# Decode attention over 65,536 keys: K and V of a head in two transfers of 64 KB per partition instead of three, over a ring of 20 + 16 chunks

## The chip, the core and the metric

The kernel runs on one core of a Trainium2 chip. The metric is the time of one execution in microseconds (us); lower is better. The kernel before has a median of 657.81 us over three runs (657.35 to 657.81).

## What is computed

One token goes through a transformer layer: layer norm, attention of 32 query heads over 8 key/value heads with 65,536 cached positions each, an output projection with a residual, a second layer norm and a gated feed-forward part with a residual. All inputs are bf16.

```python
q = (x @ wq)                                            # [1, 512] @ [512, 4096]: 32 heads of 128
scores = einsum("bhqd,bhkd->bhqk", q, k) * 128 ** -0.5  # k_cache [8, 65536, 128]
o = einsum("bhqk,bhkd->bhqd", softmax(scores), v)       # v_cache [8, 65536, 128]
h = x + o.reshape(1, 1, 4096) @ wo
h2 = h + (sigmoid(n(h) @ w_gate) * (n(h) @ w_up)) @ w_down   # n: layer norm; 512 -> 1792 -> 512
```

K and V of one head are 16 MB each, so the caches are 8 x 32 MB of the 282.33 MB that the kernel reads.

## The kernel before, in words

**Chunks and blocks.** K or V of one head is 32 chunks. A chunk is 4 KB per partition (`TC` = 16 positions of 128 bf16 values on each of 128 partitions). A block is 8 chunks (`NC`), so a head has four blocks, r = 0 to 3.

**The ring and the pieces.** K and V share one buffer, `ring`, of 32 chunks per partition. A head's K and its V come in three pieces each: chunks 0 to 11, 12 to 19 and 20 to 31 (`PIECES`), that is transfers of 6, 4 and 6 MB, or 48, 32 and 48 KB per partition. `AT` gives each piece's place in the ring.

**The DMA queue.** The SP engine issues all these transfers from one program in a fixed order (`load`, line 329): for head h, K h.0, V h-1.0, V h-1.1, K h.1, K h.2, V h-1.2. Before each, SP waits until the ring chunks that it overwrites have been read. For K these marks are one-element memsets that VectorE (DVE) does between two transposes (line 514, `F{h}.0`, `F{h}.1`, `F{h}.3`); for V they are the ends of rounds of matmuls (`PV{h}.{r}`). A transfer that must wait holds up all that stand behind it.

**K on VectorE and TensorE.** DVE transposes each chunk in blocks of 32 x 32 from `ring` into one of eight slots of the key buffer `ktw` (line 511, named `T{b}.{c}`). A piece's first transpose waits for the whole piece. A transpose into a slot also waits for the four matmuls that read the slot's last content. TensorE (PE) multiplies four chunks at a time by the query columns (`S{b}.{c}`, through the helper of line 430), and the sums of a whole head stay in four PSUM banks. After the last block come the softmax's maxima (line 518), the exponentials on ScalarE (line 557), and four transposes of the probabilities on DVE into `PT_sb` (line 567). In DVE's program these four stand behind the next head's first eight chunk transposes (`A0`, then `A4`), and after them `B0`, two small steps for the softmax's denominators that need a result of PE.

**V on TensorE.** The product with V (`pv`, also line 430) is done for head h-1 while head h is scored: rounds of eight matmuls, one round for two chunks, in PE's program behind block 0 (10 rounds) and block 3 (6 rounds). When V rounds change from one piece to the next, PE's program branches away to wait for it and comes back (`waits`).

**Start and end.** First `wq` (4 MB) comes into ring chunks 24 to 31, then K of head 0; piece K0.2 overwrites `wq` and so waits for the query projection `q` (`project_q`, to 23.3 us). At the end, V of head 7 lies in other places (`V7`); `wo` goes into `ktw`, the last piece of V comes in 2 transfers (`LAST`: 8 chunks, then 4), and the feed-forward weights follow into the ring. The output needs, in a chain, the last rounds of V, the head's output, the last rows of `wo`, the layer norm, gate and up products, `hhT` (line 831) and the down product (line 836), whose weights `wd` are the last transfers.

Of the kernel before, what the change touches and what calls it, by code (L numbers as in the profile page):

```python
# [13 lines left out]
HKV = 8  # L14
# [3 lines left out]
D = 512  # L18
# [197 lines left out]
def bass_sequential_preLN__gqa_block_cached__glu_gated_glu__decode_kernel(  # L216
# [10 lines left out]
    CH = TC * DH  # L227
    PIECES = ((0, 12), (12, 20), (20, 32))
    RING = 32 * CH
    AT = {"K": (0, 0, 8), "V": (12, 24, 20), "K0": (0, 12, 20), "V7": (0, 12, 20), "wq": 24, "wg": 0, "wd": 7}  # L230
    NF = FF // 128
# [6 lines left out]
    with ExitStack() as es:  # L238
# [78 lines left out]
        W_AT = {"wg": AT["wg"] * CH, "wu": AT["wg"] * CH + 4 * FF}  # L317
        LAST = [(20, 28), (28, 32)]

# [3 lines left out]
        def load(k, h, q, deps, sem, name, cols=None):  # L323
# [6 lines left out]

        dma("sp", lambda e: e.dma_start(ring[:, AT["wq"] * CH:(AT["wq"] + 8) * CH].rearrange("p (k n) -> p k n", k=4),
                                        A_wq.rearrange("(p k) n -> p k n", p=128)), "r0", (), "wq")
        for q in range(3):
            load("K", 0, q, ["q"] if q == 2 else (), f"r{q + 1}", f"K0.{q}")
        for h in range(1, HKV):
            load("K", h, 0, ["F0.1" if h == 1 else f"F{h - 1}.3"], "ka", f"K{h}.0")
            load("V", h - 1, 0, ["F0.3" if h == 1 else f"PV{h - 2}.3:2"], "va", f"V{h - 1}.0")
            load("V", h - 1, 1, ["F0.4" if h == 1 else f"PV{h - 2}.3"], "vb", f"V{h - 1}.1")
            load("K", h, 1, [f"F{h}.0"], "ka", f"K{h}.1")
            load("K", h, 2, [f"F{h}.1", f"PV{h - 1}.0:4"], "kb", f"K{h}.2")  # L340
            load("V", h - 1, 2, [f"PV{h - 1}.0"], "vb", f"V{h - 1}.2")
        h = HKV - 1
        load("V", h, 0, [f"F{h}.3"], "va", f"V{h}.0")
        for i, (j0, nj) in enumerate(WO):
            src = A_wo[j0 * DH:(j0 + nj) * DH, :].rearrange("(p r) n -> p (r n)", r=nj)
            dst = ktw[:, j0 * D:(j0 + nj) * D]
            dma("sp", lambda e, src=src, dst=dst: e.dma_start(dst, src), f"wo{i}", [f"PV{h - 1}.3"] if i == 0 else (), f"wo{i}")
        load("V", h, 1, (), "vm", f"V{h}.1")
        for i, cols in enumerate(LAST):
            load("V", h, 2, (), ("vb", "vl")[i], f"V{h}.2{('', 'b')[i]}", cols)  # L350
        for k, w in (("wg", B_w_gate), ("wu", B_w_up)):
            src = w.rearrange("(p k) n -> p (k n)", p=128)
            for i, (k0, k1) in enumerate(W_SPLIT[k]):
                at = W_AT[k]
                dma("sp", lambda e, at=at, w=src, a=k0 * FF, z=k1 * FF: e.dma_start(ring[:, at + a:at + z], w[:, a:z]),  # L355
                    f"{k}{i}", [f"PV{HKV - 1}.0a"] if k == "wg" else (), f"{k}.{i}")
        src = B_w_down.rearrange("(p r) n -> p r n", p=128)
# [95 lines left out]
        def project_q(e):  # L453

            e.reg_mov(reg(e, 0), addr_of(xz, 8 + 7))
            e.reg_mov(reg(e, 4), addr_of(ring, AT["wq"] * CH))
            for kt in range(1, 4):
                e.reg_alu(reg(e, kt), reg(e, 0), 2 * 16 * kt, ALU.add)
                e.reg_alu(reg(e, 4 + kt), reg(e, 4), 2 * NQ * DH * kt, ALU.add)
            with e.Fori(0, HKV):  # L460
                for kt in range(4):
                    mm_at(e, ps(1, 0, 512, 0, 8), at_reg(xz, reg(e, kt), [[4 * 16, 128], [1, 8]]),
                          at_reg(ring, reg(e, 4 + kt), [[RING, 128], [1, 512]]), False, 32)
                for kt in range(4):
                    e.reg_alu(reg(e, kt), reg(e, kt), 2, ALU.subtract)
                for kt in range(4):
                    e.reg_alu(reg(e, 4 + kt), reg(e, 4 + kt), 1024, ALU.add)
            return e.matmul(ps(1, 0, 512, 0, 8), lhsT=qz[:, 0:8], rhs=qz[:, 0:512], start=False, stop=True, skip_group_check=True)
# [31 lines left out]
        def dve_block(b):  # L500
            h, r = b // NR, b % NR
            for c in range(NC):
                n, j = b * NC + c, r * NC + c
                q = sum(j >= z for _, z in PIECES)
                at = (first_chunk("K", h, q) + j - PIECES[q][0]) * CH
                src = ring[:, at:at + CH].bitcast(fp32)
                dst = ktw[:, (n % NKT) * CH:(n % NKT + 1) * CH].bitcast(fp32)
                deps = [f"K{h}.{q}"] if j == PIECES[q][0] else []
                if r or b == 0:
                    deps.append(f"S{b - 1}.{c}" if b else None)  # L510
                op("dve", lambda e, d=dst, sr=src: e.transpose(d, sr), deps, f"T{b}.{c}", to="T")  # L511
                mark = {7: 0, 11: 1, 23: 3}.get(j, 4 if h == 0 and j == 31 else None)
                if mark is not None:
                    op("dve", lambda e, m=4 * h + mark: e.memset(scr[:, m:m + 1], 0.0), (), f"F{h}.{mark}")
# [69 lines left out]

        PARTS = {0: 10, 3: 6}

        def pv(h, r, rounds=0):
            P.part["pe"] = ("B", (h, r, rounds))
            rounds, name = rounds or PARTS[r], f"PV{h}.{r}" + "a" * (rounds == 6)
            for k in range(2):  # L590
# [78 lines left out]
        def pe_flow(e, section):  # L669
# [8 lines left out]
            w0, p0 = addr_of(ktw, W0 + NC - 1 + 127), addr_of(PT_sb, 31 * 4)  # L678
            v_at = [addr_of(ring, j * CH) for j in AT["V"]]
            step = (2 * 2 * 512, 2 - 2 * 2 * 512)  # L680
            lag = v_at[0] - addr_of(ring, AT["V7"][0] * CH)
            i_last = v_at[0] - lag
            i_first = i_last + HKV * lag
# [4 lines left out]
            e.reg_mov(p, p0)  # L688
            e.reg_alu(v, i, v_at[0], ALU.min)
            goto("part")  # L690
# [12 lines left out]
            e.reg_mov(m, 6)  # L703
            e.reg_mov(k, 4)
            away("br_eq", w, w0, "values0", lambda: section("V0"), "sums")
            e.br_ne(w, w0 - 12, on_true="next", on_false="values3")
            label("values3")
            e.reg_mov(v, v_at[2])
            e.reg_mov(m, 4)
            e.reg_mov(k, 2)  # L710
            section("V3")
            goto("sums", "values")
            pv_regs(e)

            def last_second():
                section("L")

            def waits():
                e.reg_alu(m, k, 0, ALU.add)
                e.reg_mov(k, 0)  # L720
                e.br_eq(w, w0, on_true="second", on_false="fourth")
                label("second", "waits")
                away("br_eq", i, i_last, "rows_of_o", last_second, "sums")
                section("V2")
                nc.br("sums", engines=here)
                label("fourth", "waits")
                e.br_ne(i, i_last, on_true="sums", on_false="last_rounds")
                label("last_rounds", "fourth")
                section("VL")
# [26 lines left out]
        def dve_flow(e, section):  # L756
            with e.Fori(1, HKV):
                for p in ("A0", "A4", "B0", "A1", "A2", "A3"):
                    section(p)

        P.flow = {"pe": pe_flow, "dve": dve_flow}
        P.loop_sems = {"T": ("pe", {"A": NC}), "g": ("pe", {"X": 2}), "W": ("pe", {"As": 1}), "PT": ("pe", {"V0": 1}),
                       "po": ("pe", {"V0": 1, "O": 1}), "va": ("pe", {"V0": 16}), "vb": ("pe", {"V2": 16, "V3": 16}),
                       "Q": ("dve", {"A3": NR * NC + 2}), "D": ("dve", {"A3": 6}), "E": ("dve", {"A4": 4}), "ka": ("dve", {"A3": 32}),
                       "kb": ("dve", {"A3": 16})}
        for i in range(HKV + 1):
            loop, last = 0 < i < HKV, i == HKV
            for r in range(NR):
# [5 lines left out]
                if i and r == 0:  # L774
                    transposed(i - 1)
                    P.part = {"pe": ("V0", i), "dve": ("B0", i) if loop else None}
                    denominators(i - 1)
                    op("pe", lambda e: None, [f"V{i - 1}.0", f"z{i - 1}"])
                    if last:
                        pv(i - 1, r, 6)  # L780
                    P.part["pe"] = ("L" if last else "V2", i)
                    if last:
                        project7()
                        columns()
                    op("pe", lambda e: None, [f"V{i - 1}.1"])
                    pv(i - 1, r, 4 if last else 0)
                if i and r == 3:
                    P.part["pe"] = ("V3", i)
                    op("pe", lambda e: None, [f"V{i - 1}.2"])
                    if last:  # L790
                        P.part["pe"] = ("VL", i)
                        op("pe", lambda e: None, [f"V{i - 1}.2b"])
                    pv(i - 1, r)
                    P.part["pe"] = ("O", i)
                    head_out(i - 1)
# [81 lines left out]
```

## Time and profile before

| | |
|---|---|
| median of three runs | 657.81 us (657.35 to 657.81) |
| profiled execution: its own time | 657.62 us |
| its span in the trace | 656.2 us |
| DMA traffic | 282.33 MB, mean 430 GB/s |
| PE busy, DVE busy | 436.0 us (66%), 351.2 us (54%) |
| granted TensorE clock, mean | 0.775 |
| chain that ended last: share of DMA | 65% |

The profile shows one execution on the chip. Its span runs from the first to the last instruction; the execution's own time is 1.4 us longer. A busy share is an average over the whole span and says nothing about which engine sets the end; for this the chain of waits and the slices of the DMA row are read. In a timeline, a line gives the start, the length (of several instructions run together), the engine, the source line, the operation, what it writes and reads, the count, and in brackets the idle time before it with what ended it.

### The profile page before, as it was taken

The page shows a single profiled execution, that of the slowest core. Times are in us where ns is not written, and L with a number is a line of the kernel's source. Part 1 is how long each engine was busy: PE and PEld are TensorE (multiplying, and loading weights), DVE is VectorE, ACT ScalarE, POOL GpSimd, SP SyncE. Part 2 cuts the span into 40 slices and gives each one's busy share as a digit, 9 for nine tenths or more (in the row PEclk, how much of TensorE's full clock was granted, in tenths as well). Part 3 has the DMA queues.
Part 4 walks back from the last instruction along what each step waited for, and adds up shares of the span by engine and source line. Part 5 has one row for each costly group of instructions (what it writes and reads, how often), then busy time and mean ns, then how long its engine had stood idle before and what let it go on. Part 6 is the DMA issues. An engine that isn't in the chain of part 4 may idle for free.

```text
span 656.2 us, 6248 instructions
## 1 busy us (share of the span) xinstructions
PE 436.0 (66%) x2316; PEld 69.4 (11%) x1548; DVE 351.2 (54%) x436; ACT 42.8 (7%) x114; POOL 3.6 (1%) x17
## 2 busy tenths in 40 slices
PE   2698675838658457776676477594667856775855
PEld 1100010001001010010100110010100101001212
DVE  3498836847266645647258380674536572573102
ACT  1100200020000200011000200002000020002001
POOL 1000000000000000000000000000000000000000
PEclk9798688767689587796677676985877967877777
DMA  9999999999999999999999999999999999999998
GB/s 400 431 447 431 425 424 446 437 434 426 441 431 431 431 431 442 437 434 423 423 443 431 431 437 445 437 437 431 415 431 431 431 434 434 457 431 411 439 422 341
DMA packets 8386, 282.33 MB, mean 430 GB/s; under 512 B 961, under 2 KB 962, under 8 KB 1474
## 3 DMA queue, kind: packets, MB, share of 16 engines
q1 hardware_dynamic: 8354, 282.33, 99.6%
q10 hardware_dynamic: 32, 0.00, 0.0%
HBM read 282.33 MB, written 0.00 MB: 430 GB/s over the span
## 4 chain that ended last, share of the span: by engine, by line
DMA 65%; PE 19%; DVE 12%; issue 3%; ACT 1%; SPq 0%; PEldq 0%
DMA ring<-in_A_k_cache_dram 34%; DMA ring<-in_A_v_cache_dram 23%; PE PS L430 18%; DVE ktw L511 11%; DMA ring<-in_B_w_down_dram 6%; DMA ring<-in_A_wq_dram 2%; ACT P_sb L557 1%; DVE PT_sb L567 0%; DVE M_sb L518 0%; SPq L355 0%; PE PS L551 0%; PE PS L544 0%; PEldq L171 0%; SPq L360 0%; PE PS L572 0%
## 5 line engine op out<-in xcount | busy, mean ns | idle before, releaser
L511 DVE STREAM_TRANSPOSE ktw<-ring 128x1024 f32<-128x1024 f32 x256 | 292.4, 1211 | 170.5 <-DMA ring<-in_A_k_cache_dram 170.5
L430 PE MATMUL PS<-ktw 128*128 128x512 bf16 x1024 | 293.2, 438 | 114.8 <-DVE ktw L511 106.7
L430 PE MATMUL PS<-ring,PT_sb 128*32 x1024 | 102.7, 506 | 65.4 <-PEq L171 45.1
L430 PEld LDWEIGHTS PS<-ktw 128*128 x256 | 27.2, 106 | 370.4 <-issue 258.1
L600 ACT ACTIVATE po_sb<-PS,rl 128x512 bf16<-128x512 f32 x8 | 5.5, 687 | 522.2 <-PE PS L430 522.2
L430 PEld LDWEIGHTS PS<-ring,PT_sb 128*32 x1024 | 20.7, 116 | 144.3 <-issue 142.8
L518 DVE TENSOR_REDUCE M_sb<-PS 128x1 f32<-128x512 f32 x32 | 19.9, 684 | 20.0 <-PE PS L430 20.0
L546 DVE TENSOR_REDUCE gmj<-PS 1x4 f32<-1x128 f32 x8 | 2.2, 278 | 40.2 <-PE PS L544 40.2
L557 ACT ACTIVATE P_sb<-PS,negmax 128x512 bf16<-128x512 f32 x32 | 21.5, 685 | 0.3
L567 DVE STREAM_TRANSPOSE PT_sb<-P_sb 128x512 bf16<-128x512 bf16 x32 | 20.2, 688 | 1.7 <-ACT P_sb L557 1.7
L430 PE MATMUL PS<-ring,xz 128*8 x32 | 10.0, 490 | 3.6 <-DMA ring<-in_A_wq_dram 3.6
L616 DVE TENSOR_TENSOR Lw<-O,blk_of 128x896 bf16<-128x896 bf16 (+1 forms) x2 | 1.4, 682 | 19.9 <-ACT O L606 19.9
L544 PE MATMUL PS<-identf,gm 128*1 128x128 f32 x16 | 4.5, 380 | 5.5 <-issue 3.4
L551 PE MATMUL PS<-one_f,gmrep 1*128 1x1 f32 x16 | 4.7, 358 | 5.0 <-DVE gmrep L548 5.0
L574 DVE TENSOR_REDUCE lsum<-PS 128x1 f32<-128x4 f32 x8 | 1.3, 162 | 11.9 <-PE PS L572 11.9
L475 DVE STREAM_TRANSPOSE qt<-qh 32x512 bf16<-32x512 bf16 x1 | 0.7, 699 | 12.7 <-ACT qh L472 12.7
L430 PE MATMUL PS<-ktw,O 128*1 x26 | 7.5, 457 | 0.0
L557 ACT ACTIVATION_READ_ACCUMULATOR P_sb<-PS,negmax 128x1 f32 x32 | 6.5, 203 | 0.0
L603 PE MATMUL PS<-sel_bf,po_sb 128*128 128x4 bf16 x32 | 2.1, 170 | 6.3 <-ACT po_sb L600 6.3
L411 PE MATMUL PS<-xs,xpick 16*128 16x32 bf16 x1 | 0.2, 202 | 7.5 <-DMA xs<-in_A_x_dram 7.5
L572 PE MATMUL PS<-L_sb,lsel 128*128 128x4 f32 x16 | 2.5, 229 | 3.8 <-DVE PT_sb L567 3.8
L661 DVE COPY yr<-PS 1x512 f32<-1x512 f32 x1 | 0.7, 678 | 8.1 <-PE PS L659 8.1
(88 smaller groups left out, 71.6 us busy)
## 6 DMA issues: line engine op xcount, KB each, us to landing
ring<-in_A_k_cache_dram SPq DMA_DIRECT2D x16, 6144.0 KB, 25.4
ring<-in_A_v_cache_dram SPq DMA_DIRECT2D x15, 6144.0 KB, 25.7
ring<-in_A_v_cache_dram SPq DMA_DIRECT2D x9, 4096.0 KB, 30.6
ring<-in_A_k_cache_dram SPq DMA_DIRECT2D x8, 4096.0 KB, 24.7
ring<-in_A_wq_dram SPq DMA_DIRECT2D x1, 4096.0 KB, 12.3
ktw<-in_A_wo_dram SPq DMA_DIRECT2D x1, 3584.0 KB, 14.9
ring<-in_A_v_cache_dram SPq DMA_DIRECT2D x1, 2048.0 KB, 38.5
ring<-in_B_w_gate_dram SPq DMA_DIRECT2D x1, 1792.0 KB, 30.8
```

The lines of the kernel that those rows point to most:

```text
L430: return e.add_instruction(mybir.InstMatmult(name=nc.get_next_instruction_name(), engine=mybir.EngineType.PE, ins=[rhs, lhsT], outs=[e.low ...
L511: op("dve", lambda e, d=dst, sr=src: e.transpose(d, sr), deps, f"T{b}.{c}", to="T")
L518: op("dve", lambda e, u=u: e.tensor_reduce(M_sb[:, u % 4:u % 4 + 1], ps(u % NS, 0, 512), AX.X, ALU.max), [f"S{b}.{NC - NR + k}"], f"mx{u}" ...
L544: op("pe", lambda e: e.matmul(ps(MISC, 0, 128, 0, 1), lhsT=gm[:, :], rhs=identf[:, :], start=True, stop=True), [f"gm{h}"], f"gmT{h}", to="Q")
L546: op("dve", lambda e: e.tensor_reduce(gmj[:, :], ps(MISC, 0, 128, 0, 1).rearrange("p (i a c) -> p a i c", a=4, c=NC), AX.XY, ALU.max), [f" ...
L551: op("pe", lambda e: e.matmul(ps(MISC, 128, 129), lhsT=gmrep[0:1, :], rhs=one_f[0:1, 0:1], start=True, stop=True), [f"gmrep{h}"], f"neg{h}")
L557: op("act", lambda e, b=b: e.activation(P_sb[:, (b % 4) * 512:(b % 4 + 1) * 512], ps(b % NS, 0, 512), AF.Exp, bias=negmax[:, k:k + 1], sca ...
L567: op("dve", lambda e, b=b: e.transpose(PT_sb[:, (b % 4) * 512:(b % 4 + 1) * 512], P_sb[:, (b % 4) * 512:(b % 4 + 1) * 512]), [f"E{b}"], f" ...
L572: op("pe", lambda e: e.matmul(ps(MISC, 132, 136), lhsT=lsel[:, :], rhs=L_sb[:, :], start=True, stop=True), [f"PT{NR * h + NR - 1}"], f"l{h ...
L600: op("act", lambda e: e.activation(po_sb[:, :], ps(PO, 0, 512), AF.Copy, scale=rl[:, :]), [f"PV{h}.{NR - 1}", f"rl{h}"], f"po{h}", to="po")
L603: op("pe", lambda e, t=t: e.matmul(ps(OX, 0, 4), lhsT=po_sb[:, t * 128:(t + 1) * 128], rhs=sel_bf[:, 8 * t:8 * t + 8:2], start=(t == 0), s ...
L616: op("dve", lambda e: e.tensor_tensor(Lw[i][:, :].rearrange("p (j c) -> p j c", j=n), bass.AP(tensor=O2, offset=j0, ap=[[NQ, 128], [1, n], ...
```

## The change

The pieces become two per head: chunks 0 to 15 and 16 to 31, each 8 MB or 64 KB per partition. The ring grows from 32 to 36 chunks: 20 for K and 16 for V. K's two pieces overlap there (places 0 to 15 and 4 to 19), and V's two pieces have the same 16 places. So that K's second piece can be loaded while the first is still being read, DVE takes the first piece in a turned order, chunks 4 to 15 and then 0 to 3 (`ORDER`); the mark that releases the second piece stands after the 12th transpose of a head, the one that releases the next head's first piece after the 28th. The order of issue becomes K h.0, V h-1.0, K h.1, V h-1.1. V rounds are now 8 behind block 1 and 8 behind block 3, each in two parts of 6 and 2. In DVE's program `B0` moves behind the second block's transposes. K of head 0 comes in four transfers of 8 chunks and overlaps with nothing, since `wq` now lies in `ktw`: for this, the first transpose of all waits for `q`, and no K transfer does. The last transfer pair of V becomes 12 and 4 chunks, and the feed-forward weights wait for all 8 rounds of V7's first piece instead of 6.

```diff
-    PIECES = ((0, 12), (12, 20), (20, 32))
-    RING = 32 * CH
-    AT = {"K": (0, 0, 8), "V": (12, 24, 20), "K0": (0, 12, 20), "V7": (0, 12, 20), "wq": 24, "wg": 0, "wd": 7}
+    PIECES = ((0, 16), (16, 32))
+    RING = 36 * CH
+    AT = {"K": (0, 4), "V": (20, 20), "K0": (0, 20), "V7": (0, 20), "wg": 0, "wd": 7}
+    ORDER = (*range(4, 16), *range(4), *range(16, 32))
...
-        LAST = [(20, 28), (28, 32)]
+        LAST = [(16, 28), (28, 32)]
...
-        dma("sp", lambda e: e.dma_start(ring[:, AT["wq"] * CH:(AT["wq"] + 8) * CH].rearrange("p (k n) -> p k n", k=4),
+        dma("sp", lambda e: e.dma_start(ktw[:, 0:NKT * CH].rearrange("p (k n) -> p k n", k=4),
                                         A_wq.rearrange("(p k) n -> p k n", p=128)), "r0", (), "wq")
-        for q in range(3):
-            load("K", 0, q, ["q"] if q == 2 else (), f"r{q + 1}", f"K0.{q}")
+        for q in range(2):
+            for i in range(2):
+                j0 = 16 * q + 8 * i
+                load("K", 0, q, (), f"r{2 * q + i + 1}", f"K0.{q}{'ab'[i]}", (j0, j0 + 8))
         for h in range(1, HKV):
-            load("K", h, 0, ["F0.1" if h == 1 else f"F{h - 1}.3"], "ka", f"K{h}.0")
-            load("V", h - 1, 0, ["F0.3" if h == 1 else f"PV{h - 2}.3:2"], "va", f"V{h - 1}.0")
-            load("V", h - 1, 1, ["F0.4" if h == 1 else f"PV{h - 2}.3"], "vb", f"V{h - 1}.1")
-            load("K", h, 1, [f"F{h}.0"], "ka", f"K{h}.1")
-            load("K", h, 2, [f"F{h}.1", f"PV{h - 1}.0:4"], "kb", f"K{h}.2")
-            load("V", h - 1, 2, [f"PV{h - 1}.0"], "vb", f"V{h - 1}.2")
+            load("K", h, 0, ["F0.0" if h == 1 else f"F{h - 1}.1"], "ka", f"K{h}.0")
+            load("V", h - 1, 0, ["F0.1" if h == 1 else f"PV{h - 2}.3"], "va", f"V{h - 1}.0")
+            load("K", h, 1, [f"F{h}.0"], "kb", f"K{h}.1")
+            load("V", h - 1, 1, [f"PV{h - 1}.1"], "vb", f"V{h - 1}.1")
...
-                    f"{k}{i}", [f"PV{HKV - 1}.0a"] if k == "wg" else (), f"{k}.{i}")
+                    f"{k}{i}", [f"PV{HKV - 1}.1"] if k == "wg" else (), f"{k}.{i}")
...
-                n, j = b * NC + c, r * NC + c
+                n, s = b * NC + c, r * NC + c
+                j = ORDER[s]
...
-                mark = {7: 0, 11: 1, 23: 3}.get(j, 4 if h == 0 and j == 31 else None)
+                mark = ({15: 0, 31: 1} if h == 0 else {11: 0, 27: 1}).get(s)
...
-        PARTS = {0: 10, 3: 6}
...
-                for p in ("A0", "A4", "B0", "A1", "A2", "A3"):
+                for p in ("A0", "A4", "A1", "B0", "A2", "A3"):
...
+                if i and r == 1:
                     P.part = {"pe": ("V0", i), "dve": ("B0", i) if loop else None}
                     denominators(i - 1)
                     op("pe", lambda e: None, [f"V{i - 1}.0", f"z{i - 1}"])
+                    pv(i - 1, r, 6)
+                    pv(i - 1, r, 2)
```

More of the change, by code (lines that the diff above doesn't have):

```diff
@@ L329, in load @@
             dma("sp", lambda e: e.dma_start(ring[:, at + a * CH:at + z * CH], rows[:, (a - j0) * CH:(z - j0) * CH]), sem, deps, name)
-        dma("sp", lambda e: e.dma_start(ring[:, AT["wq"] * CH:(AT["wq"] + 8) * CH].rearrange("p (k n) -> p k n", k=4),
+        dma("sp", lambda e: e.dma_start(ktw[:, 0:NKT * CH].rearrange("p (k n) -> p k n", k=4),
                                         A_wq.rearrange("(p k) n -> p k n", p=128)), "r0", (), "wq")
-        for q in range(3):
-            load("K", 0, q, ["q"] if q == 2 else (), f"r{q + 1}", f"K0.{q}")
+        for q in range(2):
+            for i in range(2):
+                j0 = 16 * q + 8 * i
+                load("K", 0, q, (), f"r{2 * q + i + 1}", f"K0.{q}{'ab'[i]}", (j0, j0 + 8))
         for h in range(1, HKV):
-            load("K", h, 0, ["F0.1" if h == 1 else f"F{h - 1}.3"], "ka", f"K{h}.0")
-            load("V", h - 1, 0, ["F0.3" if h == 1 else f"PV{h - 2}.3:2"], "va", f"V{h - 1}.0")
-            load("V", h - 1, 1, ["F0.4" if h == 1 else f"PV{h - 2}.3"], "vb", f"V{h - 1}.1")
-            load("K", h, 1, [f"F{h}.0"], "ka", f"K{h}.1")
-            load("K", h, 2, [f"F{h}.1", f"PV{h - 1}.0:4"], "kb", f"K{h}.2")
-            load("V", h - 1, 2, [f"PV{h - 1}.0"], "vb", f"V{h - 1}.2")
+            load("K", h, 0, ["F0.0" if h == 1 else f"F{h - 1}.1"], "ka", f"K{h}.0")
+            load("V", h - 1, 0, ["F0.1" if h == 1 else f"PV{h - 2}.3"], "va", f"V{h - 1}.0")
+            load("K", h, 1, [f"F{h}.0"], "kb", f"K{h}.1")
+            load("V", h - 1, 1, [f"PV{h - 1}.1"], "vb", f"V{h - 1}.1")
         h = HKV - 1
-        load("V", h, 0, [f"F{h}.3"], "va", f"V{h}.0")
+        load("V", h, 0, [f"F{h}.1"], "va", f"V{h}.0")
         for i, (j0, nj) in enumerate(WO):
@@ L347, in bass_sequential_preLN__gqa_block_cached__glu_gated_glu__decode_kernel @@
             dma("sp", lambda e, src=src, dst=dst: e.dma_start(dst, src), f"wo{i}", [f"PV{h - 1}.3"] if i == 0 else (), f"wo{i}")
-        load("V", h, 1, (), "vm", f"V{h}.1")
         for i, cols in enumerate(LAST):
-            load("V", h, 2, (), ("vb", "vl")[i], f"V{h}.2{('', 'b')[i]}", cols)
+            load("V", h, 1, (), ("vb", "vl")[i], f"V{h}.1{('', 'b')[i]}", cols)
         for k, w in (("wg", B_w_gate), ("wu", B_w_up)):
@@ L455, in project_q @@
             e.reg_mov(reg(e, 0), addr_of(xz, 8 + 7))
-            e.reg_mov(reg(e, 4), addr_of(ring, AT["wq"] * CH))
+            e.reg_mov(reg(e, 4), addr_of(ktw))
             for kt in range(1, 4):
@@ L462, in project_q @@
                     mm_at(e, ps(1, 0, 512, 0, 8), at_reg(xz, reg(e, kt), [[4 * 16, 128], [1, 8]]),
-                          at_reg(ring, reg(e, 4 + kt), [[RING, 128], [1, 512]]), False, 32)
+                          at_reg(ktw, reg(e, 4 + kt), [[KTW_ROW, 128], [1, 512]]), False, 32)
                 for kt in range(4):
@@ L507, in dve_block @@
                 dst = ktw[:, (n % NKT) * CH:(n % NKT + 1) * CH].bitcast(fp32)
-                deps = [f"K{h}.{q}"] if j == PIECES[q][0] else []
-                if r or b == 0:
-                    deps.append(f"S{b - 1}.{c}" if b else None)
+                if h == 0:
+                    deps = [f"K0.{q}{'ab'[j % 16 // 8]}"] if s in (0, 4, 16, 24) else []
+                    if s == 0:
+                        deps.append("q")
+                else:
+                    deps = [f"K{h}.{q}"] if s in (0, 16) else []
+                if r:
+                    deps.append(f"S{b - 1}.{c}")
                 op("dve", lambda e, d=dst, sr=src: e.transpose(d, sr), deps, f"T{b}.{c}", to="T")
-                mark = {7: 0, 11: 1, 23: 3}.get(j, 4 if h == 0 and j == 31 else None)
+                mark = ({15: 0, 31: 1} if h == 0 else {11: 0, 27: 1}).get(s)
                 if mark is not None:
@@ L583, in pv_regs, with pv @@
                         e.reg_alu(reg(e, i + 4), R["v"], 2 * (k * TC + 4 * tq) * 128, ALU.add)
-        PARTS = {0: 10, 3: 6}
-        def pv(h, r, rounds=0):
+        def pv(h, r, rounds):
             P.part["pe"] = ("B", (h, r, rounds))
-            rounds, name = rounds or PARTS[r], f"PV{h}.{r}" + "a" * (rounds == 6)
+            name = f"PV{h}.{r}" + "a" * (rounds == 6)
             for k in range(2):
@@ L678, in pe_flow @@
             w0, p0 = addr_of(ktw, W0 + NC - 1 + 127), addr_of(PT_sb, 31 * 4)
-            v_at = [addr_of(ring, j * CH) for j in AT["V"]]
+            v_at = addr_of(ring, AT["V"][0] * CH)
+            v_from = addr_of(ring, (AT["V"][0] + ORDER[0]) * CH)
             step = (2 * 2 * 512, 2 - 2 * 2 * 512)
-            lag = v_at[0] - addr_of(ring, AT["V7"][0] * CH)
-            i_last = v_at[0] - lag
+            lag = (AT["V"][0] - AT["V7"][0]) * 2 * CH
+            i_last = v_from - lag
             i_first = i_last + HKV * lag
@@ L688, in pe_flow @@
             e.reg_mov(p, p0)
-            e.reg_alu(v, i, v_at[0], ALU.min)
             goto("part")
@@ L703, in pe_flow, with values1 @@
             e.reg_mov(m, 6)
-            e.reg_mov(k, 4)
-            away("br_eq", w, w0, "values0", lambda: section("V0"), "sums")
+            e.reg_mov(k, 2)
+            def values1():
+                e.reg_alu(v, i, v_from, ALU.min)
+                section("V0")
+            away("br_eq", w, w0 - 4, "values1", values1, "sums")
             e.br_ne(w, w0 - 12, on_true="next", on_false="values3")
             label("values3")
-            e.reg_mov(v, v_at[2])
-            e.reg_mov(m, 4)
-            e.reg_mov(k, 2)
+            away("br_eq", i, i_last, "rows_of_o", lambda: section("L"))
+            e.reg_mov(v, v_at)
             section("V3")
@@ L713, in pe_flow @@
             pv_regs(e)
-            def last_second():
-                section("L")
             def waits():
@@ L720, in waits @@
                 e.reg_mov(k, 0)
-                e.br_eq(w, w0, on_true="second", on_false="fourth")
+                e.br_eq(w, w0 - 4, on_true="second", on_false="fourth")
                 label("second", "waits")
-                away("br_eq", i, i_last, "rows_of_o", last_second, "sums")
-                section("V2")
+                e.reg_alu(v, v, 16 * 2 * CH, ALU.subtract)
                 nc.br("sums", engines=here)
@@ L762, in bass_sequential_preLN__gqa_block_cached__glu_gated_glu__decode_kernel @@
         P.loop_sems = {"T": ("pe", {"A": NC}), "g": ("pe", {"X": 2}), "W": ("pe", {"As": 1}), "PT": ("pe", {"V0": 1}),
-                       "po": ("pe", {"V0": 1, "O": 1}), "va": ("pe", {"V0": 16}), "vb": ("pe", {"V2": 16, "V3": 16}),
-                       "Q": ("dve", {"A3": NR * NC + 2}), "D": ("dve", {"A3": 6}), "E": ("dve", {"A4": 4}), "ka": ("dve", {"A3": 32}),
+                       "po": ("pe", {"V0": 1, "O": 1}), "va": ("pe", {"V0": 16}), "vb": ("pe", {"V3": 16}),
+                       "Q": ("dve", {"A3": NR * NC + 2}), "D": ("dve", {"A3": 6}), "E": ("dve", {"A4": 4}), "ka": ("dve", {"A3": 16}),
                        "kb": ("dve", {"A3": 16})}
@@ L778, in bass_sequential_preLN__gqa_block_cached__glu_gated_glu__decode_kernel @@
                     op("pe", lambda e: None, [f"V{i - 1}.0", f"z{i - 1}"])
+                    pv(i - 1, r, 6)
+                    pv(i - 1, r, 2)
+                if i and r == 3:
                     if last:
-                        pv(i - 1, r, 6)
-                    P.part["pe"] = ("L" if last else "V2", i)
-                    if last:
+                        P.part["pe"] = ("L", i)
                         project7()
                         columns()
+                    P.part["pe"] = ("V3", i)
                     op("pe", lambda e: None, [f"V{i - 1}.1"])
[L786 to L789, printed above, removed]
+                    pv(i - 1, r, 6)
                     if last:
                         P.part["pe"] = ("VL", i)
-                        op("pe", lambda e: None, [f"V{i - 1}.2b"])
-                    pv(i - 1, r)
+                        op("pe", lambda e: None, [f"V{i - 1}.1b"])
+                    pv(i - 1, r, 2)
                     P.part["pe"] = ("O", i)
```

## The prediction

> **What bounds the kernel now.** I read the slices of the page first, then a window of the long middle, then the chain of waits, the DMA queue's own timeline, and DVE's timeline in one head.
>
> ```profile
> DMA  9999999999999999999999999999999999999998
> q1 hardware_dynamic: 8354, 282.33, 99.6%
> 12.30:600.00 587.70, 401.40 (x2019) 56.71 (x1251) 336.28 (x386) 34.62 (x95) 0.00 (x0) 0.78 1.00 434
> ```
>
> The DMA row never drops before the last slice, and from 12.3 to 600 us the 16 DMA engines are busy for a share of 1.00 at 434 GB/s. PE works 401 of these 588 us and DVE 336. So the stream of bytes sets the time, and the compute engines matter only where they are late in freeing ring space, or after the last bytes. The chain shows it too:
>
> ```profile
> 0.00 12.31 DMA ring<-in_A_wq_dram
> ...
> 162.54 28.71 DMA ring<-in_A_k_cache_dram
> ...
> 209.03 25.73 DMA ring<-in_A_v_cache_dram
> ```
>
> A 6 MB transfer needs 14.5 us (below), yet these take 25 to 29 us from issue to landing: each waits more than 10 us behind others. That queue is what the kernel lives on. The change makes transfers larger and the buffer hardly larger, so the question is whether the queue still never runs empty.
>
> **Price of a transfer.** In DVE's timeline a piece's first transpose starts when it lands. Third K pieces start 14.48 to 14.51 us after second ones (for example 176.80 and 191.28), and these are 6 MB. From first to second K piece it is 33.86 to 33.88 us, a 6 MB and two 4 MB transfers, so 4 MB takes (33.87 - 14.50) / 2 = 9.69 us. Hence 2 MB costs 4.81 us, a fixed part of about 0.05 us remains for each transfer, and 8 MB should take 19.30 us. The number of K and V transfers falls from 49 to 35: 14 x 0.05 = 0.7 us saved. With 0.03 us of scatter in the rows, the bounds are 0 and 2 us.
>
> Were transfers not overlapped, the saving would be large: the Trainium skill, "DMA: Bandwidth & Descriptors", section "Anatomy of one DMA", fits about 2.0 us plus bytes / 436e3, by which 14 fewer transfers would save 28 us. The 0.05 us between back-to-back transfers here does not bear this out; the fixed part is hidden while something is queued.
>
> What it costs when nothing is queued is seen at the start: `wq` is issued at 0.00 and lands at 12.31 us, 2.62 us more than the 9.69. I use 2.62 us as the **turn-around** from issue to landing beyond the pure transfer. The nearest other row is the 1 KB load of x on ScalarE's queue, 6.7 us to landing beside a busy stream; it is on another queue, so I take it only as the upper bound.
>
> **The new waits, head by head.** Each transfer must be issued 2.62 us before its predecessor's end, or the stream has a hole. The tightest is K h.1, which waits for 12 transposes of K h.0, with the four transposes of the probabilities among them (`A4`), while V h-1.0 is being loaded.
>
> ```profile
> 220.24 9.13 DVE L511 STREAM_TRANSPOSE ktw<-ring 128x1024 f32<-128x1024 f32 x8 [4.12 <-DMA ring<-in_A_k_cache_dram]
> 229.29 0.71 DVE L567 STREAM_TRANSPOSE PT_sb<-P_sb 128x512 bf16<-128x512 bf16 x1
> 229.31 0.06 DVE L514 MEMSET scr<- 1x1 f32 x1
> 229.92 1.86 DVE L567 STREAM_TRANSPOSE PT_sb<-P_sb 128x512 bf16<-128x512 bf16 x3
> 232.65 0.16 DVE L574 TENSOR_REDUCE lsum<-PS 128x1 f32<-128x4 f32 x1 [0.86 <-PE PS L572]
> 232.84 0.16 DVE L575 RECIPROCAL rl<-lsum 128x1 f32<-128x1 f32 x1
> 232.92 4.61 DVE L511 STREAM_TRANSPOSE ktw<-ring 128x1024 f32<-128x1024 f32 x4
> 237.47 0.06 DVE L514 MEMSET scr<- 1x1 f32 x1
> 229.42 10.91 SPq L329 DMA_DIRECT2D ring<-in_A_k_cache_dram  x2
> ```
>
> Eight transposes take 9.05 us to the start of the next operation, the four of the probabilities 2.49 us (229.29 to 231.78), four more with the mark 4.55 us (232.92 to 237.47). The denominators between them now stand behind the second block, so the 1.14 us from 231.78 to 232.92 falls away here. From the mark to SP's issue is 0.11 us (229.31 to 229.42), and from landing to first transpose 0.03 us. Sum: 0.03 + 9.05 + 2.49 + 4.55 + 0.11 = 16.2 us after K h.0 lands. With the turn-around, K h.1's data follow without a hole if 16.2 + 2.6 = 18.8 is under 19.3, V's transfer time. It is, by **0.5 us**. PE doesn't delay this: the ninth transpose needs PE to have read the first slot, and PE has the 2.5 us of the probabilities as a reserve.
>
> The others are looser. K h+1.0 waits for 12 transposes with nothing between: 0.03 + 9.05 + 4.55 + 0.11 = 13.7, a reserve of 2.9 us. V h-1.1 waits for PE: 16 transposes end 20.6 us after K h.0 lands, PE trails by 3 us at full clock (591.74 to 594.77 in the last head) and by up to 6 us if the clock is at half throughout the second block, and eight rounds take 8 to 9 us. That is 32 to 36 us against 38.6 - 2.6 = 36.0. V h.0 has 2 us or more in the same sum. In head 0 the first transpose now waits for `q` (23.3 us) and starts about 24.6 instead of 26.9 us; its last ends near 63.4 instead of 64.7, and V0.0 has to be issued by 67.7. Moving `wq` and reordering chunks therefore cost nothing, nor do the four smaller K0 transfers, which queue without waiting. So I forecast no hole in the middle.
>
> **The tail.** Here the work after the last bytes counts.
>
> ```profile
> 596.70 0.63 PE L430 MATMUL PS<-ring,PT_sb 128*32 x8 [0.34 <-issue]
> 598.57 0.63 PE L430 MATMUL PS<-ring,PT_sb 128*32 x8 [1.24 <-issue]
> ...
> 636.76 3.82 PE L430 MATMUL PS<-ring,PT_sb 128*32 x32 [6.04 <-PEq L171]
> 641.68 0.63 PE L430 MATMUL PS<-ring,PT_sb 128*32 x8 [1.10 <-DMA ring<-in_A_v_cache_dram]
> 642.65 0.63 PE L430 MATMUL PS<-ring,PT_sb 128*32 x8 [0.34 <-issue]
> ...
> 652.39 0.62 PE L836 MATMUL PS<-ring,hhT 128*1 128x128 bf16 x32 [1.29 <-DVE hhT L831]
> 653.29 0.39 PE L836 MATMUL PS<-ring,hhT 128*1 128x128 bf16 x16 [0.29 <-DMA ring<-in_B_w_down_dram]
> 653.92 0.38 PE L836 MATMUL PS<-ring,hhT 128*1 128x128 bf16 x8 [0.23 <-DMA ring<-in_B_w_down_dram]
> ```
>
> Before, PE did four rounds on the last-but-one transfer of V and two on the last. Now it does six and two, since that transfer has 12 chunks. They start 0.7 us earlier with the stream, at 636.1. Six starts 1.0 us apart put the sixth at 641.1; the branch to the last part costs 1.87 us (596.70 to 598.57), so the last two start at 642.9 and 643.9 and end at 644.5, against 643.28: 1.3 us later (1.6 at the 1.06 us per round of 636.76). The down product then starts at 653.7 instead of 652.39. It no longer waits for its weights, and its 56 matmuls take about 1.0 us (32 in 0.62): it ends at 654.7 to 655.0 instead of 654.30. The end moves by +0.4 to +0.7 us, I take **+0.5**. Unless PE's chain is shorter than this, the stream's 0.7 us brings nothing. The rest of the tail has cover: `wo` and the feed-forward weights are issued over 3 us before the stream reaches them, by the same sums.
>
> **The sum.** 657.62 us (span 656.2) + 0.5 = 658.1; the profiled execution lies 0.2 below the median, so I say 658.2. A measurement here tells about 0.2%, or 1.3 us, from no change.
>
> **Rivals.**
>
> *The wait for 12 transposes opens a hole in every head.* It decides from a turn-around of 3.1 us on, half a microsecond above the one cold start that I could read; that start had no stream beside it. For it: the reserve is 3% of a transfer. Against: a start from empty should be the slow case. Price: heads 1 to 7, so 7 x (turn-around - 3.1): at 3.6 us, 3.5 + 0.5, or 662; at the bound of 6.7 us, 25 us, or 683. Chance 0.30.
>
> *PE at half clock is late for V h-1.1.* The granted clock is 0.78 on average, and where half clock falls on the second block the reserve is 0.3 us. A miss of 1 to 2 us in half the heads gives 662 to 665. Chance 0.06.
>
> *Rows at a pitch of 64 KB load slower.* Pieces of 4 MB have rows 32 KB apart and run at 433 GB/s, the 6 MB ones with 48 KB at 434, so a power of two does no harm so far. Each 1% on 28 transfers of 19.3 us is 5.4 us: 663 or more. Chance 0.04. The Trainium skill, "DMA: Bandwidth & Descriptors", section "Latency and other measured facts", has 207 GB/s at 512 KB pitch where 214 is full, and far less at 2 MB; no run here has such a pitch, and by that 3% it would be 674.
>
> *The rows are cut in two, so that fewer transfers do not mean fewer packets.* Then the 0.7 us of the stream is lost and the tail stays: 658.8. Chance 0.04.
>
> *Faster.* The fixed part of a transfer is 0.14 us, at the rows' upper bound, and PE's tail is hidden: 14 x 0.14 = 2, or 655.8. Chance 0.04.
>
> **How the numbers follow.** The forecast has 0.52. It and the cut rows lie within 0.2% of 657.8: same 0.56. Slower is 0.30 + 0.06 + 0.04 = 0.40, faster 0.04. The likeliest case alone spans 656.9 (stream's gain kept) to 659. The range goes from there up to 664.5, which takes in holes of up to about 0.85 us per head and leaves out the heavier ones and the low end.
>
> **What would show it.** In the profile after: the DMA row full throughout; K h.1 issued about 16.2 us after the first transpose of K h.0; first transposes of successive K pieces 38.6 us apart. The forecast fails if these are further apart, if the share of DMA in the middle falls below 1.00, or if SP's issue comes late because transposes wait for PE. In the tail, six rounds, a gap near 1.2 us, two rounds; and a down product that waits for `hhT`, not for `wd`.

## The result, and the profile after

The changed kernel takes 667.96 us (median of six runs, 666.32 to 669.40) against 657.74 us for the kernel before: a ratio of 1.0155, interval 1.0145 to 1.0166. It is slower by about 10 us. The profiled execution took 666.32 us with a span of 665.0.

The slices of the page and the same long window as before:

```profile
GB/s 400 426 436 442 442 434 442 438 406 426 438 442 442 434 386 442 442 438 442 386 442 438 442 434 390 442 442 438 414 398 438 434 438 402 438 426 442 415 420 277
12.30:600.00 587.70, 359.55 (x1949) 53.96 (x1186) 332.58 (x371) 34.67 (x95) 0.00 (x0) 0.80 1.00 430
```

The mean of the window falls from 434 to 430 GB/s. The dips of the slices to 386 to 414 GB/s, about one in five, are no sign of a hole: a run without holes (below) has the same, since a packet of 64 KB is counted whole in the slice where it starts. The share of busy DMA engines still says 1.00, so that sign of the prediction misses the loss. A packet that waits for its first bytes counts as busy: behind the empty queue of the second experiment the first packets last 3.1 us on average, against 2.4 in a full queue. The chain of waits shows the place (start, length, what):

```profile
86.37 23.82 DMA ring<-in_A_k_cache_dram
...
123.91 24.93 DMA ring<-in_A_k_cache_dram
...
164.92 23.50 DMA ring<-in_A_k_cache_dram
...
202.14 24.93 DMA ring<-in_A_k_cache_dram
...
243.14 24.05 DMA ring<-in_A_k_cache_dram
...
280.91 24.94 DMA ring<-in_A_k_cache_dram
```

Start plus length is a landing. These are K1.1 (110.19), K2.0 (148.84), K2.1 (188.42), K3.0 (227.06), K3.1 (267.19) and K4.0 (305.85). From K h.1 to K h+1.0 it is 38.65 us, two full transfers. From K h.0 to K h.1 it is 39.6 and 40.1, and over the seven heads 38.67 to 40.70 us, 39.73 on average; in head 4 (38.67) next to nothing is lost. DVE's timeline in head 2, and then SP's issue of K2.1:

```profile
148.86 9.13 DVE L517 STREAM_TRANSPOSE ktw<-ring 128x1024 f32<-128x1024 f32 x8 [7.19 <-DMA ring<-in_A_k_cache_dram]
157.91 2.45 DVE L573 STREAM_TRANSPOSE PT_sb<-P_sb 128x512 bf16<-128x512 bf16 x4
160.29 5.76 DVE L517 STREAM_TRANSPOSE ktw<-ring 128x1024 f32<-128x1024 f32 x5
164.81 0.06 DVE L520 MEMSET scr<- 1x1 f32 x1
```

```profile
164.92 0.33 SPq L330 DMA_DIRECT2D ring<-in_A_k_cache_dram  x1
```

The eight transposes, the probabilities and the mark follow as forecast, and K2.1 is issued 16.08 us after K2.0 landed, against 16.2. So the release came on time by the plan, and the stream still had a hole behind it in six of the seven heads.

### The profile page after: what moved, and what is told of

The parts are those of the page before. It is cut to its first block, busy times and chain, and to the rows that moved or that the text cites. A ratio compares the mean times of both kernels' runs of the same rounds, so it can differ in the third digit from the quotient of the medians.

```text
span 665.0 us, 6197 instructions
## 1 busy us (share of the span) xinstructions
PE 399.3 (60%) x2316; PEld 68.5 (10%) x1548; DVE 350.2 (53%) x427; ACT 42.9 (6%) x114; POOL 3.6 (1%) x17
## 3 DMA queue, kind: packets, MB, share of 16 engines
q1 hardware_dynamic: 6338, 282.33, 98.9%
## 4 chain that ended last, share of the span: by engine, by line
DMA 59%; DVE 33%; PE 5%; issue 3%; ACT 0%; SPq 0%; PEldq 0%
DMA ring<-in_A_k_cache_dram 56%; DVE ktw L517 30%; DMA ring<-in_A_v_cache_dram 4%; PE PS L430 3%; DVE PT_sb L573 2%; PE PS L822 0%; PE PS L671 0%; PE PS L840 0%; DVE hh L832 0%; PE PS L626 0%; PE PS L636 0%; ACT po_sb L604 0%; DVE yr L665 0%; DVE hhT L835 0%; PE PS L391 0%
## 5 line engine op out<-in xcount | busy, mean ns | idle before, releaser
L430 PE MATMUL PS<-ktw 128*128 128x512 bf16 x1024 | 280.8, 420 | 178.4 <-DVE ktw L517 170.8
L430 PE MATMUL PS<-ring,PT_sb 128*32 x1024 | 80.9, 409 | 45.8 <-issue 41.9
L524 DVE TENSOR_REDUCE M_sb<-PS 128x1 f32<-128x512 f32 x32 | 19.9, 684 | 19.3 <-PE PS L430 19.3
L430 PE MATMUL PS<-ktw,xz 128*8 x32 | 8.4, 429 | 3.6 <-DMA ktw<-in_A_wq_dram 3.6
L490 ACT ACTIVATE PS<-zcol 128x512 f32<-128x512 bf16 x8 | 5.0, 621 | 0.0
```

Of the source, the lines that this page charges most:

```text
L430: return e.add_instruction(mybir.InstMatmult(name=nc.get_next_instruction_name(), engine=mybir.EngineType.PE, ins=[rhs, lhsT], outs=[e.low ...
L490: op("act", lambda e: e.activation(ps(PO, 0, 512), bass.AP(tensor=zcol, offset=0, ap=[[1, 128], [0, 512]]), AF.Copy), ["zcol"] if h == 0 e ...
L524: op("dve", lambda e, u=u: e.tensor_reduce(M_sb[:, u % 4:u % 4 + 1], ps(u % NS, 0, 512), AX.X, ALU.max), [f"S{b}.{NC - NR + k}"], f"mx{u}" ...
```

## The experiments

All are edits of the changed kernel; ratios are to the kernel before, and "..." marks what is left out of an edit (such as the waits and semaphores of an added transfer). "Release" is the time from the landing of K h.0 to the issue of K h.1; V h-1.0, in between, lasts 19.3 us.

**The release 2.4 us earlier.** The probabilities' transposes move behind the second block.

```diff
-                if i and r == 0:
-                    transposed(i - 1)
                 if i and r == 1:
+                    transposed(i - 1)
...
-                for p in ("A0", "A4", "A1", "B0", "A2", "A3"):
+                for p in ("A0", "A1", "A4", "B0", "A2", "A3"):
```

> The four transposes of the probabilities move behind the second block's chunk transposes, so the mark that releases K h.1 comes 2.4 us earlier, about 13.7 instead of 16.1 us after K h.0 lands. Transfers, places and order stay as in the changed kernel. Theory A (late release: K h.1 is issued too shortly before its predecessor ends, and the stream has a hole of about 1.1 us in each of heads 1 to 7): successive landings of K h.0 and K h.1 come back to 38.7 us, and the time to 658.5 us, with 1 to 1.5 us left for the longer tail; between 657.5 and 660. Theory B (rows of 64 KB load slower or their fixed cost is higher): nothing changes, 666 to 669 us. Theory C (PE is late for V h-1.1): nothing changes, or it gets worse, since PE waits for the probabilities.

Measured: 659.18 us (657.90 to 659.89), ratio 1.002 (1.001 to 1.0029). K h.0 to K h.1 is 38.60 us in every head. The window is back at 434 GB/s, and the slices dip as before:

```profile
GB/s 401 429 439 455 447 399 431 447 447 447 391 439 447 447 439 395 443 447 447 435 395 447 447 447 431 399 447 447 447 431 399 447 447 447 431 399 447 421 431 315
12.30:600.00 587.70, 365.97 (x2011) 55.09 (x1243) 335.46 (x377) 34.67 (x95) 0.00 (x0) 0.80 1.00 434
```

Nearly the whole loss is gone with the same transfers in the same places, so theory A holds, and the 64 KB rows are not the cause.

**The release far too late**, to see an empty queue in the middle of a run.

```diff
-                mark = ({15: 0, 31: 1} if h == 0 else {11: 0, 27: 1}).get(s)
+                mark = ({15: 0, 31: 1} if h == 0 else {15: 0, 27: 1}).get(s)
```

> The mark that releases K h.1 stands after 16 instead of 12 transposes, so it is issued about 20.7 us after K h.0 lands, when its predecessor has already ended and the queue is empty. This measures the turn-around of an empty queue in the middle of the run. If it is the 2.62 us of the cold start, K h.1 lands 20.7 + 2.6 + 19.3 = 42.6 us after K h.0, 4.0 us per head above the 38.6 of a full queue, and the time is about 686 us. If every late issue costs 4.4 us, as the issue-to-landing times of the changed kernel (23.7 us on average) suggest, it lands at 44.4 and the time is about 698 us. Theory B: 668, no change.

Measured: 685.77 us (two runs, 685.32 and 686.21), ratio 1.0427 (1.0407 to 1.0448). DVE's timeline gives the landings of K1.0 and K1.1, SP's the issue of K1.1:

```profile
70.25 9.13 DVE L517 STREAM_TRANSPOSE ktw<-ring 128x1024 f32<-128x1024 f32 x8 [0.88 <-DMA ring<-in_A_k_cache_dram]
112.53 14.94 DVE L517 STREAM_TRANSPOSE ktw<-ring 128x1024 f32<-128x1024 f32 x13 [18.22 <-DMA ring<-in_A_k_cache_dram]
```

```profile
90.81 0.33 SPq L330 DMA_DIRECT2D ring<-in_A_k_cache_dram  x1
```

From 90.81 to 112.50 it is 21.7 us, or 2.4 us beyond the transfer; over the seven heads 2.4 to 2.7. The turn-around of an empty queue is therefore what the cold start said (2.6). The issue-to-landing times of 22.6 to 24.6 us in the changed kernel do not contradict it: there the new transfer also waits for the end of its predecessor.

**The same release by another way.** Probabilities behind the second block as in the first run, the mark behind the 14th transpose (index 13 in the program).

> The transposes of the probabilities behind the second block as in the first of these runs, but the mark after 14 instead of 12 chunk transposes, which puts the release of K h.1 back to 16.0 us after K h.0 lands. Theory A: the time of the release counts and not what DVE did before it, so this is the changed kernel again, 666 to 669 us, with K h.0 to K h.1 at 39 to 41 us. If the probabilities' transposes disturb in another way (for instance by delaying PE), it is about 658.5 us.

Measured: 666.63 us (663.12 to 668.87), ratio 1.0132 (1.0092 to 1.0172); K h.0 to K h.1 38.8 to 40.2 us, 39.67 on average. The time of the release counts, not what DVE did before it.

**More work queued ahead of the late release.** The free quarter of K h.1 is issued without a wait.

```diff
-            load("K", h, 1, [f"F{h}.0"], "kb", f"K{h}.1")
+            load("K", h, 1, (), "kc", f"K{h}.1b", (28, 32))
+            load("K", h, 1, [f"F{h}.0"], "kb", f"K{h}.1", (16, 28))
...
```

> K h.1 comes in two transfers: chunks 28 to 31 (2 MB), whose places are free, are issued without a wait right behind V h-1.0, and chunks 16 to 27 (6 MB) at the mark as before, at 16.1 us. The release is as late as in the changed kernel, but 4.8 us more of other work is queued ahead of it. Theory A: the hole is gone, and seven more transfers cost 0.05 us each: 659 us, between 657.5 and 660. Theory B: rows are 48 KB and 16 KB in K h.1 and 64 KB elsewhere, so a quarter of the loss at most goes away: 664 to 669 us.

Measured: 659.00 us, ratio 1.0018 (1.0009 to 1.0028), K h.0 to K h.1 38.70 us. The release is as late as in the changed kernel; the cover in the queue alone closes the hole.

**How much lead is needed.** Probabilities behind the second block, the mark behind the 13th transpose.

> Probabilities' transposes behind the second block, mark after 13 chunk transposes: release 14.9 us after K h.0 lands, 4.4 us before its predecessor ends. Theory A in the form that a turn-around of 2.6 to 3.5 us has to be covered: no hole, as with the mark after 12: 658 to 660 us, all landings of K 38.6 apart. If a busy stream needs much more lead (over 4.4 us): some of the hole is there, 661 to 666 us.

Measured: 659.30 us, ratio 1.0029 (1.0017 to 1.0041), no hole: 38.59 us in all heads. And from the other side, the changed kernel with its mark behind the 14th:

> The changed kernel with the mark after 14 instead of 12 chunk transposes: release of K h.1 18.3 us after K h.0 lands, 1.0 us before its predecessor ends. With the turn-around of an empty queue (2.4 to 2.6 us from issue to landing beyond the transfer), a hole of 1.5 us per head: 658.7 + 7 x 1.5 = 669 us. If the spread between the DMA engines adds to it as in the changed kernel, where that sum gives 0 and 1.1 us was lost per head: about 2.6 us per head, 677 us.

Measured: 669.41 us, ratio 1.0181 (1.0166 to 1.0197); K h.0 to K h.1 40.15 us. That is the empty queue's sum, not more. Put together, each a mean over heads 1 to 7 of one trace (the lead is 19.3 - release, the sum is release + 2.6 - 19.3, and the hole is what K h.0 to K h.1 exceeds 38.60 by):

| release, us | lead before the predecessor's end | hole by the sum | hole measured |
|---|---|---|---|
| 13.7 | 5.6 | none | 0.00 |
| 14.9 | 4.4 | none | 0.00 |
| 16.0 | 3.3 | none | 1.07 |
| 16.1 (changed kernel) | 3.2 | none | 1.13 |
| 18.3 | 1.0 | 1.6 | 1.55 |
| 20.6 | -1.3 | 3.9 | 3.87 |

The sum is right where the queue runs empty, and wrong where it nearly does. The two means of 1.07 and 1.13 hide a wide spread: at the changed kernel's release, the same within 0.01 us in all heads, one head lost 0.07 us and the others 0.75 to 2.10.

**Are packets the reason?** First V h-1.0 in two transfers of 32 KB rows, then also K h.1:

```diff
-            load("V", h - 1, 0, ["F0.1" if h == 1 else f"PV{h - 2}.3"], "va", f"V{h - 1}.0")
+            load("V", h - 1, 0, ["F0.1" if h == 1 else f"PV{h - 2}.3"], "vc", f"V{h - 1}.0a", (0, 8))
+            load("V", h - 1, 0, (), "va", f"V{h - 1}.0", (8, 16))
...
-            load("K", h, 1, [f"F{h}.0"], "kb", f"K{h}.1")
+            load("K", h, 1, [f"F{h}.0"], "kb", f"K{h}.1", (16, 24))
+            load("K", h, 1, (), "kc", f"K{h}.1b", (24, 32))
...
```

> The changed kernel with V h-1.0 in two transfers of 8 chunks (32 KB rows) issued together, so that the packets in flight when K h.1 is issued last 1.2 instead of 2.4 us; release and bytes as in the changed kernel. Theory P (an engine that is busy takes up new work only at the end of a packet, so that long packets make some engines late and spread them): the lead of 2.4 us is enough, holes mostly go, 658.5 to 661 us. Theory A without that (the lead alone counts): as the changed kernel, 665 to 669 us.

> The changed kernel with V h-1.0 and K h.1 in two transfers each of 8 chunks, issued together, so that on both sides of the late release every row is 32 KB as in the 4 MB pieces of the kernel before; release and places as in the changed kernel. Theory A (the lead of the release counts, whatever the rows): 666 to 670 us, K h.0 to K h.1 at 39 to 41 us. Theory B (rows of 64 KB cause the loss where they meet the release): 659 to 661 us.

Measured: 668.68 us, ratio 1.018 (1.0151 to 1.0209), and 666.83 us, ratio 1.014 (1.0123 to 1.0157). Both have the changed kernel's holes (39.71 and 39.74 us on average), although a packet of 32 KB lasts 1.2 us. Theory P falls, and theory B a second time.

**The tail.** The first run still lost 1.5 us. A finer last piece of V7 should have given it back (8, 4 and 4 chunks, rounds of 4, 2 and 2, with the branches in PE's program for it).

```diff
-        LAST = [(16, 28), (28, 32)]
+        LAST = [(16, 24), (24, 28), (28, 32)]
...
-                    pv(i - 1, r, 6)
+                    pv(i - 1, r, 4 if last else 6, "a")
                     if last:
+                        P.part["pe"] = ("VM", i)
+                        op("pe", lambda e: None, [f"V{i - 1}.1b"])
+                        pv(i - 1, r, 2, "b")
                         P.part["pe"] = ("VL", i)
-                        op("pe", lambda e: None, [f"V{i - 1}.1b"])
+                        op("pe", lambda e: None, [f"V{i - 1}.1c"])
...
```

> The probabilities' transposes behind the second block, and the end of V7's second piece in three transfers of 8, 4 and 4 chunks, with PE's rounds in parts of 4, 2 and 2 that wait for one each, as the kernel before had it. Theory A with the tail's share as predicted (two more rounds after the last-but-one transfer): the last two rounds end 1.2 us earlier than in the first run of this study, the down product waits for its weights again, and the stream's saving of 0.6 to 0.7 us shows: 657.1 us, 0.1% below the kernel before; between 656.7 and 657.6. If what the first run still loses against the kernel before is not the tail, it stays at 658.5 to 659.5 us.

Measured: 659.45 us, ratio 1.003 (1.0019 to 1.0042): no gain. PE's timeline of the first run, behind the last head's denominators, and then the start of these rounds in this run say why:

```profile
612.36 5.78 PE L430 MATMUL PS<-ring,PT_sb 128*32 x48 [3.09 <-PEq L171]
...
624.91 7.32 PE L430 MATMUL PS<-ktw,O 128*1 x26
...
633.22 2.02 PE L671 MATMUL PS<-one_f,yr 1*128 1x1 f32 x8 [0.77 <-DVE yr L665]
635.97 1.59 PE L430 MATMUL PS<-ring,PT_sb 128*32 x12 [0.73 <-PEq L171]
```

```profile
635.33 3.44 PE L430 MATMUL PS<-ring,PT_sb 128*32 x32
```

PE waits 3.1 us for V7's first piece, which has 16 chunks now, and then has work up to 635.2; the next rounds begin at 635.97. With the finer last piece, its first 8 chunks land at 630.7 and find PE busy: the rounds begin at 635.33, straight after the work before them. So V7's first piece has to be finer as well (12 and 4 chunks; this alone was not run):

```diff
-        load("V", h, 0, [f"F{h}.1"], "va", f"V{h}.0")
+        load("V", h, 0, [f"F{h}.1"], "va", f"V{h}.0", (4, 16))
+        load("V", h, 0, (), "vc", f"V{h}.0b", (0, 4))
...
```

> As the fifth run (probabilities' transposes behind the second block, V7's last piece in 8, 4 and 4 chunks), and V7's first piece comes in 12 and 4 chunks, so that PE starts its rounds at 610 instead of 612 us, and the output projection of the first 28 heads ends 2 to 3 us earlier than its 635 us there. Theory T (PE is busy without a break from the landing of V7's first piece to the end, so that a finer last piece alone gains nothing): now the four rounds run from 631 to 635, the last two end near 643 us, the down product waits for its weights, and the time is 657.0 us, 0.1% below the kernel before; 656.7 to 658. If the extra branches in PE's program eat it: 658 to 659.5 us.

Measured: 657.44 us (657.20 to 658.03) against 657.63, ratio 0.9998 (0.9989 to 1.0007). The 1.7 us of the tail are back, and the version equals the kernel before; it does not beat it by anything that can be told. Its down product still waits for `hhT`, not for its weights, against what I had expected. Part of the tail hangs on the granted clock, as the windows of the down product show, first of the first run, then of the run with only the last piece finer:

```profile
653.70:654.80 1.10, 0.95 (x56) 0.76 (x56) 0.04 (x1) 0.04 (x1) 0.00 (x0) 1.00 0.00 0
```

```profile
654.40:656.20 1.80, 1.66 (x56) 1.37 (x56) 0.03 (x2) 0.03 (x1) 0.00 (x0) 0.50 0.00 0
```

The same 56 matmuls take 0.95 us at a granted clock of 1.00 and 1.66 us at 0.50. Once PE sets the end, this goes into the time. That it makes the 2 us between runs of the first experiment is argued, not shown.

## Why the prediction was wrong

The forecast was 658.2 us with a range up to 664.5; measured 667.96.

- **What bounds the kernel, and the tightest wait: right.** The release of K h.1 was named as the tightest and its time came out as 16.1 us against 16.2. K h+1.0 and V cause no hole (38.65 us throughout), so the rival of PE at half clock was wrong.
- **The price of a transfer: right.** K h.0 to K h+1.0 takes 77.28 us without holes (first run), against 77.37 before (V landings from 157.36 to 544.21 us in five heads): 0.6 us for seven heads, forecast 0.7. The 28 us by the Trainium skill ("DMA: Bandwidth & Descriptors", "Anatomy of one DMA") are not borne out. The Trainium skill fits its 2.0 us there for transfers that GpSimd issues, and these are issued by SP; the figure is near the 2.4 us of the empty queue alone.
- **The step that failed: "if 16.2 + 2.6 = 18.8 is under 19.3".** The turn-around of 2.6 us is right for a queue that is empty (2.4 in the second run), but it is not the lead that a running stream needs; the argument that a start from empty should be the slow case was wrong. A lead of 3.2 us lost 1.13 us per head, 3.3 lost 1.07, and 4.4 nothing. So what is safe lies between 3.3 and 4.4, and the reserve of 0.5 us was in truth a deficit of 0.1 to 1.2 us. Seven heads make 7.9 us. Why the running stream needs more is not shown.
- **The first rival had the right place and the wrong law.** It priced the hole at 7 x (turn-around - 3.1); the turn-around measured by itself, 2.4 us, would give none. It had 0.30, and the range stopped at 0.85 us per head.
- **The tail: right in the mechanism, too small.** In the first run's trace, without holes, the last two rounds end at 644.5 us as forecast, and the span is 0.4 us above before (forecast 0.5). The median of its runs is 1.5 us above. In the changed kernel's trace 8.7 us (666.32 against 657.62) minus 7.9 leave 0.8 us where 0.5 was forecast; without the stream's gain of 0.6 that is a tail of 1.4 against 1.2. There the rounds take longer:

```profile
643.96 3.65 PE L430 MATMUL PS<-ring,PT_sb 128*32 x32 [0.43 <-PEq L171]
...
650.88 2.08 PE L430 MATMUL PS<-ring,PT_sb 128*32 x16 [1.34 <-issue]
...
662.17 0.95 PE L840 MATMUL PS<-ring,hhT 128*1 128x128 bf16 x56 [1.12 <-DVE hhT L835]
```

From the first of the eight rounds to the end of the last it is 9.0 us instead of the 8.4 forecast. The last two explain most of it: their 16 matmuls are busy for 2.08 us at a granted clock of 0.50, against 1.26 us at 1.00 in the first run. The down product waits for `hhT`, as forecast. That PE had hardly any idle time before them, because the larger first piece of V7 lands later, the prediction had missed.
- **Pitch of 64 KB, and rows cut in two: wrong.** Without holes the stream has full rate, and the DMA packets of SP's queue fall from 8354 to 6338, which is 14 transfers with one packet per row: 128 rows and 16 packets of 4 bytes each make 144, and 14 x 144 = 2016.

## What to carry to other kernels

Where a stream is the bound, a transfer has to be issued well before its predecessor ends, and the lead that an empty queue needs is not enough; here 4.4 us was safe, 3.3 us was not. Larger transfers in the same buffer save a fixed part of 0.05 us each and take away whole transfers of cover. Two mends closed the hole: to move other work behind the release, or to split off the part whose place is free and queue it without a wait. Even with the finer tail, the larger transfers then only equal the kernel before (657.44 against 657.63 us).

## What the runs showed of the hardware

A release that comes a little too late does not only cost its hole, it also pulls the 16 DMA engines apart. In a window of 12 us cut into 40 slices, a packet seems to be counted in the slice where it starts; a 64 KB packet lasts 2.4 us, or 8 slices. The changed kernel in head 1 before its first late release, and in head 2 after two of them:

```profile
GB/s 1966 655 0 0 0 0 0 874 1966 655 0 0 0 0 0 874 1966 655 0 0 0 0 0 874 1748 874 0 0 0 0 0 874 1529 1092 0 0 0 0 0 655
```

```profile
GB/s 218 1311 655 874 218 218 0 0 218 1311 655 874 218 218 0 0 218 1092 874 874 218 218 0 0 218 874 1092 874 218 218 0 0 218 874 1092 874 218 218 0 0
```

At first the engines start their packets within 3 slices of each other, later over 6, and they stay so while the queue is full. The first run, without holes, still has them within 3 slices there:

```profile
GB/s 1311 655 0 0 0 0 0 1311 1311 874 0 0 0 0 0 1311 1311 874 0 0 0 0 0 1092 1529 874 0 0 0 0 0 1092 1529 874 0 0 0 0 0 874
```

A landing is that of the last engine, so the release that hangs on it comes later for the first ones, which run dry sooner. In the run with the release at 18.3 us, where all engines run dry, they are together again:

```profile
GB/s 0 437 1748 1311 0 0 0 0 0 218 1966 1311 0 0 0 0 0 218 1966 1311 0 0 0 0 0 0 2185 1311 0 0 0 0 0 0 1966 1311 218 0 0 0
```

This fits the table: the sum holds with the engines together and fails with them apart. But the first late release, in head 1 of the changed kernel, already cost 1.3 us (39.90 us from K1.0 to K1.1) with the engines still together. The single packets of the traces show a second part. Behind an empty queue (release at 20.6 us) every engine starts its first packet 1.0 to 2.0 us after the issue, in all seven heads. In head 1 of the changed kernel the last packets of V0.0 end 2.4 to 2.9 us after the issue; 13 of the 16 engines go on almost at once, but three are late, the last of them starting 3.5 us after the issue with a first packet of 3.1 us, and the landing waits for these. In head 4, which lost next to nothing, every engine that had run dry has started by 1.8 us after the issue. So an engine that still has work can take up the next transfer later than an idle one. Why, and why not in every head, stays open; the length of the packets is not the reason.
